# The first stage of a Fourier-and-SwiGLU kernel: an input transfer, matmul order and small sign operations moved

## The chip, the cores and the metric

The kernel runs on one core of a Trainium2 chip. The metric is the device time of one execution in microseconds; the median of three runs is given, and one further execution was taken by the hardware profiler. A core has a tensor engine (PE; its weight loads are listed as PEld), a vector engine (DVE, VectorE), a scalar engine (ACT, ScalarE), GpSimd (POOL) and a sync engine (SP) that issues most transfers. Each engine works through its own queue in order and waits for the others by semaphores.

## The reference

`x` has 8 batches of 3008 rows and 256 columns. Its two-dimensional Fourier transform is taken in each batch and the real part goes through a SwiGLU block of width 1536:

```python
X = np.fft.fft(x, axis=1)
X = np.fft.fft(X, axis=2)
x = X.real.reshape(B * S, D)
g = x @ w_gate
v = x @ w_val
return (g / (1 + np.exp(-g)) * v) @ w_out
```

## The kernel before

**The idea.** The transforms are matrix products with cosine and sine tables that the kernel makes itself. The transform along the columns is folded into the weights: `Wp` and `Wq` are the gate and value weights times a cosine and a sine matrix (`CD`, `SDt`), and `Wm` is `Wq` with a factor for the mirrored rows. The transform along the rows uses the symmetries of the tables: rows that stand opposite each other are added and subtracted first ("folding"), in quarters of a batch, so that a batch needs a fraction of the products. What comes out is held in two bf16 tiles per block of up to 512 rows, `Pt` (even part) and `Qt` (odd part); a row and its mirrored row come from `Pt` and `Qt` with the sum and the difference.

**Units.** The work behind the first stage is a list of units (t, f): row block t and 128 of the 1536 columns, f from 0 to 11. In the blocks whose kind is "w" (block 0, all of it) a unit is: gate product (`Wp` times `Pt`, then `Wq` times `Qt`, L1033), value product likewise, silu on ACT (L1068), the product `hp` of silu and value on DVE (L1071); then `Wm` times `Qt` is added to gate and value in place (L1033 again), silu (L1089), and the product `hm` (L1092). So a unit's second value product has to wait until L1071 has read the first. The output product is L1297. A small planner in the kernel (`Sched`) takes the units' operations with the costs written beside them and due times and works out one order for each engine ahead of time; the order is then fixed. The costs that it is given don't change with what an operation's function issues.

**The first stage** (up to about 18 us) is written out by hand. It loads batch 0, makes the tables, folds, and does the first half of batch 0's row transform so that block 0 can start.

- The rows of a batch quarter are cut in two parts, "A" (128 rows) and "C" (the other 60, and the middle rows). Part A comes into `XA`, part C into `XC0`. Falling rows have to be turned round; batch 0 does that on PE: a placing matrix (`putA`, `putC`, made by an iota and a compare on POOL, L411 and L412, `more_iotas` and L415) times the rows (L442). `XC0` is cleared by ACT (L300), then filled by SP's transfers (L274, L277) and by one small transfer from POOL's queue, L416: the middle rows, 4 KB.
- The folding of part C is on DVE: L449 and L450 (`cross_halves`), L460 (`half_fold`), L454 (`ends`); then L588 makes a part of the odd rows of A (`EOb`).
- PE's row products go into four accumulators, `acc[eo][q]`, eo even or odd, q the column half: `half_folded` (L485, part A), `folded_c` (L490, part C), `row0` (L634, the zero row). `even_copy` (L514, ACT) copies the accumulator of column half 0, and `first_puts` (L652, DVE) adds and subtracts it from that of half 1 and writes `Pt` (eo 0) or `Qt` (eo 1).
- `first_w` (L502) makes the first 512 columns of `Wp` and `Wq`; ACT and DVE copy them out (L505).
- Weights come by POOL's queue, `load_w` (L403): it converts to bf16 on the way. The parts for later columns are turned into `Wp` and `Wq` among the units (`weight_op`: L1519 on PE, casts L1522, L1525 and L1528, the `Wm` part on POOL, L1534).
- `heads` (L464, L465, POOL) and `row_signs` (L366, L367, POOL), with the two small products of L676, make the coefficients of single columns and rows: the signs of part C. `turn_signs` (L355 to L357, DVE) makes four signs per partition, `turn_sign`, which are read at L1586 when the second half of the odd table is made from the first half.

Among the units of block 0 stand the operations that make the odd tables (`before`, L1636): `turns` (L373, POOL), `angles` (L377, DVE), `magnitude` (L381, DVE), sine and cosine (L384, L387, ACT), the quarter rows of part A (L1564 to L1568, POOL). `magnitude_op(0)` and `magnitude_op(1)` are added at unit 3, each with a cost of 0.35.

Of the kernel before, what the change touches and what calls it, by code (L numbers as in the profile page):

```python
# [16 lines left out]
Alu = mybir.AluOpType  # L17

@with_exitstack
def kernel(  # L20
# [8 lines left out]
    nc = tc.nc  # L29
    B, M, D = x.shape  # L30
# [5 lines left out]
    R = M // 4  # L36
# [16 lines left out]
    NCR = GH - P  # L53
# [43 lines left out]
    Ec0 = mEc[:, 4:8].rearrange("p (a q d) -> p a q d", a=2, q=2)  # L97
# [10 lines left out]
    sgn = const.tile([P, 1], F32, name="sgn")  # L108
    nsgn = const.tile([P, 1], F32, name="nsgn")
# [15 lines left out]
    rrO = XA.rearrange("p a q d -> p (a q d)")[:, 4 * T:4 * T + 4 * GH].rearrange("p (c q n) -> p c q n", c=2, q=2)  # L125
# [5 lines left out]
    def rows_at(b, row, ap):  # L131
        return bass.AP(tensor=x.tensor, offset=(b * M + row) * D, ap=ap)
# [84 lines left out]
    def coef_a(b):  # L217
        if b not in coefA:
            coefA[b] = (cp.tile([P, 2, 2, 2, P + 1], BF16, name="CEa"),
                        cp.tile([P, 2, 2, 2, P], BF16, name="BBa"))  # L220
        return coefA[b]

    def stack(b):
        if b not in stacks:
            stacks[b] = stp.tile([P, 4 * ND], BF16, name="St")
        return stacks[b]
# [11 lines left out]
    pts = nc.gpsimd.tensor_scalar  # L238
# [8 lines left out]
    XC0 = tp.tile([P, 4, 2, D], F32, name="XC0")  # L247
# [58 lines left out]
    def more_iotas():  # L306
        nc.gpsimd.memset(putC, -1.0)
        for hi in range(2):
            pm = 64 * hi + NCR
            nc.gpsimd.iota(putC[:, pm - NCR:pm], pattern=[[-2 * LC, NC_], [2, LC]], base=2 * (NCR - LC) + hi, **iota)  # L310
# [42 lines left out]
    def turn_signs():  # L353
        n_ = turn_sign.bitcast(I32)
        vts(n_, mm_, scalar1=0.5, scalar2=0.25, op0=Alu.mult, op1=Alu.add)  # L355
        vts(n_, n_, scalar1=1, scalar2=None, op0=Alu.bitwise_and)
        vts(turn_sign, n_, scalar1=-2.0, scalar2=1.0, op0=Alu.mult, op1=Alu.add)  # L357
# [7 lines left out]
    def row_signs():  # L365
        pts(sgo, pc, scalar1=float(NCR), scalar2=-2.0, op0=Alu.is_equal, op1=Alu.mult)  # L366
        pts(sgo, sgo, scalar1=1.0, scalar2=sgn, op0=Alu.add, op1=Alu.mult)  # L367
# [3 lines left out]
    def turns(t1, kf, ch):  # L371
        for i in range(2):
            pts(t1[:, i, :], kf, scalar1=mM[:, 2 * ch + i:2 * ch + i + 1], scalar2=1.0, op0=Alu.mult, op1=Alu.mult)  # L373
# [6 lines left out]
    def magnitude(ra, rr):  # L380
        vts(ra.bitcast(I32), rr.bitcast(I32), scalar1=0x7FFFFFFF, scalar2=None, op0=Alu.bitwise_and)  # L381
# [16 lines left out]
    def load_w(c, only):  # L398
        for i, src in ((0, moe_w_gate), (1, moe_w_val)):
            if i not in only:  # L400
                continue
            w_ = src.rearrange("(no p) f -> p no f", p=P)[:, :, c * T:(c + 1) * T]
            nc.gpsimd.dma_start(out=Wraw[i][:, :, (c - 1) * T:c * T] if c else W0[i], in_=w_)  # L403
# [3 lines left out]
    BBc = stack(0)[:, 0:8 * P].rearrange("p (q e k d) -> p q e k d", q=2, e=2, k=2)  # L407
# [3 lines left out]
    nc.gpsimd.iota(putA, pattern=[[-LA, NA], [1, LA]], base=JA - 1, **iota)  # L411
    pts(putA, putA, scalar1=pcol, scalar2=1.0, op0=Alu.is_equal, op1=Alu.mult)  # L412
    turns(ti[1], kf, 1)
    more_iotas()
    pts(putC, putC, scalar1=pcol, scalar2=1.0, op0=Alu.is_equal, op1=Alu.mult)  # L415
    nc.gpsimd.dma_start(out=XC0[NCR:64 + NCR + 1:64, 2:4, 0], in_=rows_at(0, 0, [[2 * R * D, 2], [R * D, 2], [1, D]]))  # L416
    ce_angle = [[tp.tile([P, 2, NCE], F32, name=f"{nm}{ch}") for nm in ("rr", "ra")] for ch in range(2)]
    tp.tile([P, 4404], F32, name="pad")

# [42 lines left out]
    def heads(ev, od, CE):  # L462

        ptt(CE[:, :, 0, 0, -1:], ev, od, op=Alu.add)  # L464
        ptt(CE[:, :, 0, 1, -1:], ev, od, op=Alu.subtract)  # L465
# [9 lines left out]
    def set_cols(ps, tab, a):  # L475
        if a % 2:
            return (ps[:, 0:2 * GH + 2].rearrange("p (t n) -> p t n", t=2),
                    tab[:, 0:2 * NCE].rearrange("p (t n) -> p t n", t=2)[:, :, 0:GH + 1])
        return ps[:, 0:NCE], tab[:, 0:NCE]

    def half_folded(eo, a0, first, qs=(0, 1)):
        for q in qs:
            for a in range(a0, a0 + 2):
                dst, rhs = set_cols(acc[eo][q], Tab[:, 0, q, eo], a)
                nc.tensor.matmul(dst, EOb[:, eo, a, q, :], rhs, start=first and a == a0, stop=False, skip_group_check=True)  # L485

    def folded_c(eo, a, first=False):
        for q in range(2):
            dst, rhs = set_cols(acc[eo][q], Tab[:, 1, q, eo], a)
            nc.tensor.matmul(dst, EB[:, eo, a, q, :], rhs, start=first and a == 0, stop=a == 1, skip_group_check=True)  # L490
# [21 lines left out]
    def even_copy(eo):  # L512
        od = odp.tile([P, NCE], F32, name="od")
        nc.scalar.copy(od, acc[eo][0][:, 0:NCE])  # L514
        return od
# [70 lines left out]
    half_fold(1, EB[:, 1, 1], FC[:, 1], psC[1])  # L586
    for i in range(2):
        vtt(EOb[:, 1, 0:2, i], EOA[1][0][:, :, i], EOA[1][1][:, :, i], op=Alu.add)  # L588
    heads(Ec0[:, 0], Ec0[:, 1], CEc)
    load_w(1, (1,))  # L590
    half_folded(0, 2, False)
    folded_c(0, 0)
    copies = [first_w(0, k, 1, one_bank(k)) for k in range(2)]
# [31 lines left out]
    def row0(b, q, ps):  # L625
        if b:
            for k, (c, e) in enumerate(((0, E0), (0, E1), (1, slice(0, NCE)))):
                nc.tensor.matmul(ps[:, e], Z0[:, q, k, :], Tab[:, c, q, 0, e], start=False, stop=True,  # L628
                                 skip_group_check=True)
            return  # L630
        CE = coef_a(b)[0]
        for c, head in ((0, CE[:, q, 0, :, P:P + 1]), (1, CEc[:, q, 0])):
            for k, e in ((0, E0), (1, E1)):
                nc.tensor.matmul(ps[0:1, e], head[:, k, :], Tab[:, c, q, 0, e], start=False, stop=True,  # L634
                                 skip_group_check=True)
# [11 lines left out]
    def first_puts(eo, od, tiles):  # L647
        for c0, s0, minus in ((0, 1, 0), (GH, 0, 1), (G, GH + 1, 0), (G + GH, GH + 1, 1)):
            for t, off, src, w in pieces(c0, GH):
                if t in tiles:  # L650
                    s_ = slice(s0 + src, s0 + src + w)
                    vtt(pq_tiles(t)[eo][:, off:off + w], acc[eo][1][:, s_], od[:, s_], op=SUMS[minus])  # L652
        if 1 in tiles:
            vtt(last[eo][:, 0:1], acc[eo][1][:, 0:1], od[:, 0:1], op=Alu.add)
# [3 lines left out]
    first_puts(0, od0, (0, 1))  # L658
    for c in copies:
        c()  # L660
    half_folded(1, 0, False)
    for i in range(2):
        row0(0, i, acc[1][i])
        if i == 0:
            od1 = even_copy(1)
# [2 lines left out]
    first_puts(1, od1, (0,))  # L668
    copies[1]()
    first_puts(1, od1, (1,))  # L670
    turn_signs()
    tmp_ctx.close()
    first_ctx.close()
    row_signs()
    for k in range(2):
        pts(BBc[:, :, 1, k, 0:1], Ec0[:, 1 - k], scalar1=(nsgn, sgn)[k], scalar2=1.0, op0=Alu.mult, op1=Alu.mult)  # L676
    nc.gpsimd.iota(kfO, pattern=[[4, GH]], base=1, **iota)
    nc.gpsimd.memset(sel[0:1, :], 1.0)

# [355 lines left out]
    S = Sched()  # L1035
# [513 lines left out]
    raO = SDf.rearrange("p a d -> p (a d)")[:, 0:4 * GH].rearrange("p (c q n) -> p c q n", c=2, q=2)  # L1549
# [4 lines left out]
        S.add("DVE", 0.75, lambda: angles(rrO[:, ch], kfO, ch, turned), r=[(("A",), "pre"), (("kfO",), 0)], w=[(("rr",), ch)])  # L1554

    def magnitude_op(ch):
        S.add("DVE", 0.35, lambda: magnitude(raO[:, ch], rrO[:, ch]), r=[(("rr",), ch), (("A",), "pre")],
              w=[(("ra",), ch), (("fold",), "F")])

    def quarters_op():  # L1560
# [72 lines left out]
    def odd_op(i):  # L1633
        S.add("POOL", 1.4, lambda: odd_table(i // 2, i % 2), r=[(("Tab",), ("o", 1))], w=[(("Tab",), "k")])

    before = {0: [lambda: angle_op(0)], 1: [lambda: angle_op(1)], 2: [lambda: weight_op(1, 0)], 3: [lambda: weight_op(1, 1), lambda: magnitude_op(0), lambda: magnitude_op(1)],  # L1636
              4: [lambda: weight_op(2, 0), lambda: cosine_op(0)], 6: [quarters_op, odd_ends_op], 5: [lambda: weight_op(2, 1), lambda: cosine_op(1)],
              7: [lambda: sine_op(0), rows_op], 8: [lambda: sine_op(1)], 9: [weigh_op, lambda: second_half_op(0), lambda: second_half_op(1)],
# [56 lines left out]
    for i, u in enumerate(units):  # L1695
# [25 lines left out]
        if i == RESCALE:  # L1721
            state["scaled"] = True
            S.add("ACT", 1.3, lambda: nc.scalar.activation(Wm[:, 1], Wm[:, 1], AF.Copy, scale=-0.5),
                  r=[(("Wm",), (fc, 1)) for fc in range(3)], w=[(("Wm",), 1)])
# [58 lines left out]
```

## Time and profile before

| | us |
|---|---|
| median of three runs | 598.26 |
| the three runs | 597.51, 598.26, 598.62 |
| profiled execution, its own time | 597.96 |
| span of the profiled execution (first to last instruction) | 596.2 |
| PE busy | 590.3 (99%) |
| DVE / ACT / POOL busy | 569.2 / 553.6 / 533.1 |
| first matmul of a unit (L1033) starts | 18.26 |

The granted TensorE clock is 1.00 in every stage. A row of the timeline gives the start in us from the beginning of the span, the duration (of the whole group where it says xN), the engine, the line, the operation, output and input tiles with their shapes, and in brackets the idle time of the engine just before and what ended it. A row of the waits gives the waiting engine and line, what it waited for, the us in total, how often, and the longest. In the chain of the work that ended last each row is a piece with its start and length; "issue" is time in which the profile shows nothing that the engine waited for.

### The profile page before, as it was taken

The page shows a single profiled execution, that of the slowest core. Times are in us where ns is not written, and L with a number is a line of the kernel's source. Part 1 is how long each engine was busy: PE and PEld are TensorE (multiplying, and loading weights), DVE is VectorE, ACT ScalarE, POOL GpSimd, SP SyncE. Part 2 cuts the span into 40 slices and gives each one's busy share as a digit, 9 for nine tenths or more (in the row PEclk, how much of TensorE's full clock was granted, in tenths as well). Part 3 has the DMA queues.
Part 4 walks back from the last instruction along what each step waited for, and adds up shares of the span by engine and source line. Part 5 has one row for each costly group of instructions (what it writes and reads, how often), then busy time and mean ns, then how long its engine had stood idle before and what let it go on. Part 6 is the DMA issues. An engine that isn't in the chain of part 4 may idle for free.

```text
span 596.2 us, 12375 instructions
## 1 busy us (share of the span) xinstructions
PE 590.3 (99%) x4001; PEld 388.7 (65%) x4001; DVE 569.2 (95%) x1063; ACT 553.6 (93%) x1071; POOL 533.1 (89%) x491
## 2 busy tenths in 40 slices
PE   8999999999999999999999999999999999999997
PEld 5456666666666666666666666666666666666686
DVE  8989999999999999999999999999999999999993
ACT  8768989999999899999999999999999999999995
POOL 8989999999999999999899998999889868687782
PEclk9999999999999999999999999999999999999999
DMA  8966772756243255275225122063121103202212
GB/s 244 166 219 234 189 230 71 195 165 220 83 151 126 70 144 132 54 254 165 81 79 171 37 63 64 19 182 113 47 63 37 47 19 89 66 29 63 60 54 81
DMA packets 61086, 68.17 MB, mean 114 GB/s; under 512 B 6760, under 2 KB 48684, under 8 KB 61022
## 3 DMA queue, kind: packets, MB, share of 16 engines
q1 hardware_dynamic: 57438, 64.44, 36.1%
q0 software_dynamic: 3216, 2.36, 2.8%
q8 instruction: 31, 0.51, 0.4%
q10 hardware_dynamic: 368, 0.59, 0.3%
q14 instruction: 33, 0.27, 0.1%
HBM read 40.21 MB, written 35.43 MB: 127 GB/s over the span
## 4 chain that ended last, share of the span: by engine, by line
PE 95%; DMA 1%; POOL 1%; SPq 1%; DVE 0%; ACT 0%; issue 0%; ACTq 0%; POOLq 0%
PE o L1297 40%; PE g L1033 27%; PE v L1033 21%; PE g L1471 2%; PE o L1471 2%; PE v L1297 1%; DMA XC<-in_x_dram 1%; DMA out_dram<-ev 1%; PE o L1519 1%; POOL t L373 0%; PE g L628 0%; PE o L628 0%; SPq L1310 0%; PE b L502 0%; PE b L490 0%
## 5 line engine op out<-in xcount | busy, mean ns | idle before, releaser
L1244 POOL TENSOR_TENSOR hm<-sv 128x1024 bf16<-128x1024 f32 (+2 forms) x137 | 254.7, 1862 | 32.7 <-ACT sv L1220 16.8
L1236 DVE SCALAR_TENSOR_TENSOR sv<-es,v 128x512 f32<-128x512 f32 (+2 forms) x262 | 174.5, 672 | 6.2 <-PE v L1033 4.3
L1297 PE MATMUL o<-Wo,hm 128*128 128x256 bf16 (+1 forms) x1128 | 163.7, 273 | 0.0
L1297 PE MATMUL o<-Wo,hp 128*128 128x256 bf16 (+1 forms) x1104 | 161.1, 272 | 0.0
L1247 DVE TENSOR_TENSOR hp<-sp,v 128x512 bf16<-128x512 f32 (+2 forms) x228 | 152.0, 673 | 1.8 <-PE v L1033 1.0
L1297 PEld LDWEIGHTS <-hm 128*128 128x128 bf16 (+2 forms) x1140 | 111.9, 98 | 58.0 <-issue 0.6
L1297 PEld LDWEIGHTS <-hp 128*128 128x128 bf16 (+2 forms) x1140 | 111.9, 98 | 55.4 <-issue 0.6
L1220 ACT ACTIVATE sv<-g 128x512 f32<-128x512 f32 (+2 forms) x181 | 118.4, 672 | 3.7 <-PE g L1033 3.2
L1145 ACT ACTIVATE sp<-g 128x512 f32<-128x512 f32 (+2 forms) x181 | 111.6, 618 | 6.1 <-PE g L1033 4.5
L1033 PE MATMUL g<-Pt,Wp 128*128 128x512 bf16 (+2 forms) x288 | 107.5, 374 | 0.0
L1033 PE MATMUL v<-Pt,Wp 128*128 128x512 bf16 (+2 forms) x288 | 106.2, 374 | 0.0
L1033 PE MATMUL g<-Qt,Wq 128*128 128x512 bf16 (+2 forms) x288 | 105.4, 375 | 0.0
L1106 ACT ACTIVATE v<-bc,w 128x512 f32<-128x512 bf16 (+2 forms) x139 | 99.7, 721 | 1.7 <-DVE sv L1236 0.9
L1170 DVE SCALAR_TENSOR_TENSOR es<-bc,w,v 128x512 f32<-128x512 bf16 (+2 forms) x135 | 98.1, 734 | 2.1
L1168 ACT ACTIVATE es<-v 128x512 f32<-128x512 f32 (+2 forms) x139 | 85.4, 617 | 3.3 <-PE v L1033 1.5
L1033 PE MATMUL g<-Qt,Wm 128*128 128x512 bf16 (+2 forms) x195 | 73.1, 376 | 0.0
L1033 PEld LDWEIGHTS <-Wp 128*128 128x128 bf16 x576 | 56.3, 98 | 25.2 <-issue 0.3
L1149 DVE SCALAR_TENSOR_TENSOR sg<-bc,w,g 128x512 f32<-128x512 bf16 (+2 forms) x93 | 67.5, 726 | 1.6 <-PE g L1033 1.4
L1253 POOL TENSOR_TENSOR hp<-sp,pp 128x512 bf16<-128x512 f32 (+1 forms) x46 | 57.1, 1245 | 8.0 <-ACT pp L1250 7.8
L1220 ACT ACTIVATE sv<-sg 128x512 f32<-128x512 f32 (+2 forms) x93 | 63.4, 693 | 0.5 <-POOL hp L1253 0.5
L1213 DVE SCALAR_TENSOR_TENSOR sg<-sg,g 128x512 f32<-128x512 f32 (+2 forms) x93 | 61.8, 665 | 0.2
L1033 PEld LDWEIGHTS <-Wq 128*128 128x128 bf16 x437 | 42.7, 98 | 28.4 <-issue 1.3
(201 smaller groups left out, 781.8 us busy)
## 6 DMA issues: line engine op xcount, KB each, us to landing
out_dram<-ev SPq DMA_DIRECT2D x96, 128.0 KB
XA<-in_x_dram SPq DMA_DIRECT2D x30, 256.0 KB
tA<-in_x_dram SPq DMA_DIRECT2D x28, 256.0 KB
XA<-tA SPq DMA_DIRECT2D x14, 512.0 KB
XC<-in_x_dram SPq DMA_DIRECT2D x28, 120.0 KB
tC<-in_x_dram SPq DMA_DIRECT2D x28, 120.0 KB
XC<-tC SPq DMA_DIRECT2D x6, 480.0 KB
bc<-br SPq DMA_DIRECT2D x19, 128.0 KB
```

Source lines behind the costliest of these rows:

```text
L1033: nc.tensor.matmul(ps[:, :n], Wt[:, gv, fs], src[:, :n], start=start, stop=stop, skip_group_check=True)
L1106: nc.scalar.activation(T_[kv][:, :w], bc[t][:, :w], AF.Copy, scale=w0[:, 1, f:f + 1])
L1145: nc.scalar.activation(sp_to()[:, :w], T_[kg][:, :w], AF.Silu)
L1149: nc.vector.scalar_tensor_tensor(T_[keg][:, :w], bc[t][:, :w], w0[:, 0, f:f + 1], T_[kg][:, :w], op0=Alu.mult, op1=Alu.add)
L1168: nc.scalar.activation(T_[kes][:, :w], T_[kv][:, :w], AF.Copy, scale=2.0 if on_pool(u) > 1 else 1.0)
L1170: nc.vector.scalar_tensor_tensor(T_[kes][:, :w], bc[t][:, :w], w0[:, 1, f:f + 1], T_[kv][:, :w], op0=Alu.mult, op1=Alu.add)
L1213: nc.vector.scalar_tensor_tensor(T_[kgm][:, :w], T_[keg][:, :w], 2.0, T_[kg][:, :w], op0=Alu.mult, op1=Alu.subtract)
L1220: nc.scalar.activation(sv()[:, f % 2, w - 1::-1, 1], T_[kgm if by_dve else kg][:, :w], AF.Silu)
L1236: nc.vector.scalar_tensor_tensor(sv()[:, f % 2, w - 1::-1, 0], T_[kes][:, :w], 2.0, T_[kv][:, :w], op0=Alu.mult, op1=Alu.subtract)
L1244: nc.gpsimd.tensor_tensor(hts_(t)[1][:, f - 1:f + 1, :w], sv()[:, :, :w, 1], sv()[:, :, :w, 0], op=Alu.mult)
L1247: nc.vector.tensor_tensor(hts_(t)[0][:, f, :wp], T_[ksp][:, :wp], T_[kv][:, :wp], op=Alu.mult)
L1297: nc.tensor.matmul(st["ps"][:n, j, :], hts[t][minus][:, f, c:c + n], Wo[:, f, :], start=(f == 0), stop=(f == nF - 1))
```

## The change

Four things are moved; nothing is computed otherwise.

1. L416, the middle rows' transfer, is issued on POOL before `more_iotas` and L415, not behind them.
2. `half_folded(1, 0, ...)` is called for one column half at a time, each followed by its `row0`; before, both halves came first. The copy `even_copy(1)` stays behind the first `row0`.
3. `row_signs` is issued before `heads`, and the two products of L676 between the fourth and the last two of `load_w`'s transfers; before, all four stood at the end of the stage, ahead of the iota `kfO`.
4. `turn_signs` is no longer at the end of the stage; its three DVE operations are issued right behind the first magnitude (L381, channel 0), at unit 3, within the same planned operation.

```diff
     turns(ti[1], kf, 1)
+    nc.gpsimd.dma_start(out=XC0[NCR:64 + NCR + 1:64, 2:4, 0], in_=rows_at(0, 0, [[2 * R * D, 2], [R * D, 2], [1, D]]))
     more_iotas()
     pts(putC, putC, scalar1=pcol, scalar2=1.0, op0=Alu.is_equal, op1=Alu.mult)
-    nc.gpsimd.dma_start(out=XC0[NCR:64 + NCR + 1:64, 2:4, 0], in_=rows_at(0, 0, [[2 * R * D, 2], [R * D, 2], [1, D]]))
...
+    row_signs()
     heads(Ec0[:, 0], Ec0[:, 1], CEc)
     load_w(1, (1,))
+    for k in range(2):
+        pts(BBc[:, :, 1, k, 0:1], Ec0[:, 1 - k], scalar1=(nsgn, sgn)[k], scalar2=1.0, op0=Alu.mult, op1=Alu.mult)
     half_folded(0, 2, False)
...
-    half_folded(1, 0, False)
     for i in range(2):
+        half_folded(1, 0, False, (i,))
         row0(0, i, acc[1][i])
         if i == 0:
             od1 = even_copy(1)
...
-    turn_signs()
     tmp_ctx.close()
     first_ctx.close()
-    row_signs()
-    for k in range(2):
-        pts(BBc[:, :, 1, k, 0:1], Ec0[:, 1 - k], scalar1=(nsgn, sgn)[k], scalar2=1.0, op0=Alu.mult, op1=Alu.mult)
     nc.gpsimd.iota(kfO, pattern=[[4, GH]], base=1, **iota)
...
     def magnitude_op(ch):
-        S.add("DVE", 0.35, lambda: magnitude(raO[:, ch], rrO[:, ch]), r=[(("rr",), ch), (("A",), "pre")],
+        S.add("DVE", 0.35, lambda: (magnitude(raO[:, ch], rrO[:, ch]), ch or turn_signs()), r=[(("rr",), ch), (("A",), "pre")],
               w=[(("ra",), ch), (("fold",), "F")])
```

## The prediction

> **What bounds the kernel now.** I read the head of the profile's page first, then the waits of the tensor engine, then the chain of work that ended last, then the timeline of the first 31 us engine by engine.
>
> ```profile
> span 596.2 us, 12375 instructions
> PE 590.3 (99%) x4001; PEld 388.7 (65%) x4001; DVE 569.2 (95%) x1063; ACT 553.6 (93%) x1071; POOL 533.1 (89%) x491
> ...
> PE v L1033 <- DVE hp L1071: 0.5, 1, 0.5
> PE b L490 <- DVE EOf L460: 0.4, 1, 0.4
> ```
>
> PE is the bound. The list of its waits has four rows (line, releaser, us in total, times, longest); three belong to the first stage, as the second one shown here, and the only one behind it is the 0.5 us at L1033. So a microsecond by which PE's stream comes earlier or later before about 31 us stands unchanged in the end time: behind it PE has no idle time that could swallow a delay, and none that a gain could come from. The question is only how the start and the first units move. Of them these rows (start, us, engine, line) carry the argument:
>
> ```profile
> 6.10 0.20 POOL L307 MEMSET putC<- 128x128 f32 x1
> ...
> 6.92 0.94 POOL L415 TENSOR_SCALAR putC<-putC,pcol 128x128 f32<-128x128 f32 x1
> 7.81 0.81 POOL L416 DMA_DIRECT2D XC<-in_x_dram  x1
> ...
> 7.81 3.83 DMA XC<-in_x_dram
> 11.64 0.40 issue
> ```
>
> The chain hangs on POOL's queue up to the issue of the middle rows (L416), then on that transfer, and VectorE stands idle for 0.40 us, from 11.64, until it starts L449 at 12.04.
>
> **Part 1, the transfer ahead of the matrix.** L416 starts at 6.10 in place of 7.81, ahead of L307, the two iotas and L415. These four come 0.81 later: L415 ends at 8.67 in place of 7.86. The matmul that reads putC starts at 9.41 (row below), so 0.74 us of cover are left; the weight issue L403 behind the five stays where it is. No other queue's order changes. With the same 4.2 us (7.81 to 12.04) the rows are there at 10.3, before VectorE is free at 11.64. It can then start L449 at about 11.6: gain at most 0.45 us, nothing if another of the XC transfers, whose landing no row shows, is as late. I take 0.4, because the chain names this transfer and no other.
>
> The Trainium skill, page "SBUF — State Buffer", section "SBUF: two separate sides", warns that GpSimd cannot write the descriptors of a transfer while VectorE runs an operation on both of its ports. By it L416 at 6.10, beside VectorE's angle operations, could be stretched to about 7.7 and the gain would be near 0.1 in place of 0.4; that is rival 3 below by another way.
>
> **Part 2, by column half.**
>
> ```profile
> 9.41 1.96 PE L442 MATMUL b<-XC,putC 128*128 128x512 f32 x4
> ...
> 15.87 0.83 PE L485 MATMUL b<-Tab,EOb 128*128 128x377 bf16 x4
> 16.63 0.33 PE L634 MATMUL b<-Tab,CEa 128*1 128x189 bf16 x2
> ...
> 17.13 0.33 PE L634 MATMUL b<-Tab,CEc 128*1 128x189 bf16 x2
> 17.39 0.60 PE L502 MATMUL b<-W,CD 128*128 128x512 bf16 x2
> ...
> 18.26 0.57 PE L1033 MATMUL g<-Pt,Wp 128*128 128x480 bf16 x2
> 17.67 0.35 DVE L652 TENSOR_TENSOR Qt<-b,od 128x188 bf16<-128x188 f32 x1 [0.34 <-ACT od L514]
> ```
>
> The same eight and four matmuls run in another order, so that the copy L514 can start two L485 matmuls (some 0.4 us) earlier. But L652 reads both halves, and PE's last L634 pair ends at 17.46 (17.13 + 0.33): at most 17.67 - 17.50 = 0.17 is won. Against it, the step from the last L634 pair to L502 took 0.26 where a pair takes 0.17 (three in 17.13 - 16.63), and the new order has two such changes of kind more: 0.18 lost. Net nothing, bounds 0.17 either way. Both parts together: L1033 starts at about 17.9 in place of 18.26, 0.35 gained (bounds 0.1 and 0.6).
>
> **Part 3, row signs by the heads.**
>
> ```profile
> 15.20 0.20 POOL L464 TENSOR_TENSOR CEc<-mEc 128x2 bf16<-128x2 f32 x1 [0.54 <-DVE mEc L454]
> ...
> 17.94 0.25 POOL L366 TENSOR_SCALAR sgo<-pc 128x1 f32<-128x1 f32 x1
> ...
> 19.01 0.28 POOL L677 IOTA EOf<- 128x188 f32 x1
> ...
> 15.68 0.73 POOL L403 DMA_DIRECT2D XA<-in_moe_w_val_dram  x1
> ...
> XA<-in_moe_w_val_dram POOLq DMA_DIRECT2D x1, 256.0 KB, 6.5
> ...
> 23.02 0.59 PE L1519 MATMUL o<-XA,CD 128*128 128x512 bf16 x2
> ```
>
> Four POOL instructions (L366, L367, L676 twice) fill 17.94 to 19.01, 1.07 us. Their new place begins in the 0.54 us in which POOL waits for the heads, so some 0.4 are hidden, and the last two weight issues (L403 again) come about 0.65 later. A landing later by these 0.65 costs at most a part of the lead that PE has by then, nothing against before. What follows on POOL (L677, L678, L509) comes about 0.5 us earlier. The weight issue ahead of them stays at 15.68; with its 6.5 us it lands at 22.2, and L1519 reads it at 23.02: PE cannot be more than 0.8 us ahead of before there, whatever else is won.
>
> **Part 4, turn signs.** This decides.
>
> ```profile
> 3.60 1.17 DVE L377 SCALAR_TENSOR_TENSOR rr<-kf,mM,t 128x377 f32<-128x377 f32 x2
> ...
> 5.64 1.44 DVE L377 SCALAR_TENSOR_TENSOR rr<-kf,mM,t 128x377 f32<-128x377 f32 x2
> ...
> 19.55 0.60 DVE L355 TENSOR_SCALAR turn_sign<-mEc 128x4 int32<-128x4 f32 x1
> 20.18 0.63 DVE L356 TENSOR_SCALAR turn_sign<-turn_sign 128x4 int32<-128x4 int32 x1
> 20.85 0.36 DVE L357 TENSOR_SCALAR turn_sign<-turn_sign 128x4 f32<-128x4 int32 x1
> 21.12 1.21 DVE L1071 TENSOR_TENSOR hp<-sg,v 128x480 bf16<-128x480 f32 x2
> ...
> 24.15 0.64 DVE L1092 TENSOR_TENSOR hm<-sg,v 128x480 bf16<-128x480 f32 x1
> ...
> 25.84 0.64 DVE L381 TENSOR_SCALAR SDf<-XA 128x376 int32<-128x376 int32 x1
> 26.40 0.64 DVE L1071 TENSOR_TENSOR hp<-sg,v 128x480 bf16<-128x480 f32 x1
> 26.96 0.34 DVE L381 TENSOR_SCALAR SDf<-XA 128x376 int32<-128x376 int32 x1
> ...
> 19.43 1.36 POOL L509 TENSOR_SCALAR Wm<-Wq,m 128x512 bf16<-128x512 bf16 x2
> 20.77 1.60 POOL L373 TENSOR_SCALAR XA<-EOf,mM 128x188 int32<-128x188 f32 x4
> ...
> 24.84 0.68 POOL L1534 TENSOR_SCALAR Wm<-Wq,m 128x512 bf16<-128x512 bf16 x1 [0.74 <-ACT Wq L1528]
> 25.50 0.72 POOL L1564 TENSOR_TENSOR BBa<-Af,XA 128x256 bf16<-128x256 f32 x1
> ...
> 26.23 0.83 POOL L1565 TENSOR_TENSOR BBa<-XA,Af 128x256 bf16<-128x256 f32 x1
> 27.04 0.82 POOL L1534 TENSOR_SCALAR Wm<-Wq,m 128x512 bf16<-128x512 bf16 x1
> 27.83 1.26 POOL L1567 TENSOR_TENSOR BBa<-Fc 128x512 bf16<-128x512 f32 x1
> ...
> 27.09 0.36 PE L1033 MATMUL v<-Qt,Wm 128*128 128x480 bf16 x1
> ```
>
> Four elements a partition need no 0.6 us. Set beside POOL's rows the reason shows: L356 ends at 20.82, just behind the second L509 (20.79); L355 ends at 20.15, behind the first of the pair (19.43 + 0.68 = 20.11); L357 ends at 21.21, one L373 (0.40) behind 20.77. Each sign operation lasts until the POOL instruction beside it is done. The two L381 agree: the same work takes 0.64 with L1564 beside it (ends 26.22) and 0.34 when L1565 is nearly done (27.06). And as each sign operation reads the one before, POOL's next instruction has started when the next one comes, and it waits for all of that too.
>
> The Trainium skill, page "SBUF — State Buffer", section "SBUF: two separate sides", says so too: VectorE in a two-port mode and GpSimd hold a shared port exclusively, for a whole instruction, and the other blocks fully. The trace agrees, with the ends named above. By that rule moving the three operations saves nothing where POOL is busy.
>
> What is removed: 1.57 us of VectorE (19.55 to 21.12), and PE's wait for L1071, the 0.5 of the waits list. L1071 then starts at about 19.45 (19.55 less the 0.35, and a quarter of a microsecond for ScalarE's silu, an estimate), and PE runs 0.8 us ahead of before, as far as the weights let it, up to 26 us.
>
> What is added: L381, three signs and then L1071, whose result PE's L1033 at 27.09 waits for (26.40 + 0.64 = 27.04). VectorE shows no idle time in its rows from 21.12 to 26.96, so a delay here is paid by PE at once. The cost of the three: beside an idle POOL next to nothing, and no more than three times the 0.34 that L381 took for 376 elements; beside a busy one at most what is left of one POOL instruction and two or three whole ones. Walking it: with L1071 at 19.45 the cast and the angles (L377, four of them, beside POOL's L373 now, where the pair at 5.64 took 1.44 against 1.17 at 3.60) end between 22.6 and 23.3, and the first L381 comes, 1.69 behind L1092, at 24.2 to 24.9 in place of 25.84. POOL's L1534 waits for ScalarE's cast, hence for PE, and comes at 24.0; from there L1564, L1565, L1534 and L1567 follow without a gap. With L381 at 24.9: it waits for L1564 and ends at 25.6; L1565 then ends at 26.3 and the first sign behind it, L1534 at 26.9 and the second, L1567 at 28.1 and the third. L1071 starts at 28.1, not 26.40: **1.7 us late**. With L381 at 24.2 everything is one instruction earlier, the last wait is for L1534, and L1071 starts at 26.9: 0.5 late. I take the first, for the angles stood beside POOL's L373 in the rows named and lost time there. Up to 2.0 is possible, if L381 comes later still.
>
> PE then has lost its lead and 1.7 us more at that matmul, and there is nothing behind it where it could catch up.
>
> **Sum.** The profiled execution took 597.96 (span 596.2 and 1.76 around it). The start's 0.35, the 0.5 and the lead up to 0.8 are used up in the wait for L1071; what remains is its lateness: 597.96 + 1.7 = 599.66, so **599.7 us**. The median of the runs shown is 598.26, 0.30 above the profiled execution, and they reach from 597.51 to 598.62; 0.3 of this goes into the range at the upper end.
>
> **The rivals.**
> 1. *One POOL instruction fewer in the way*: the angles are not held up, or a sign operation gets through at the small memset between L1564 and L1565. L1071 is 0.1 to 0.5 late: 598.1 to 598.5. For it: the walk misses such a gap by less than 0.1 us. Against: in the old place all three lost.
> 2. *Faster*: the signs run beside an idle POOL. The row of L1534 shows 0.74 us in which POOL waits for ScalarE; if L381 and the signs fall there, they cost 1.0 at most, and L1071 is still ahead of before. It decides where L381 starts before POOL's L1534 has its data. PE keeps 0.6 to 0.9 of its lead: 597.1 to 597.4. Against: that L1534 comes at 24.0, 0.8 earlier with PE's lead, and VectorE, which comes 0.9 to 1.6 earlier, would have to reach L381 1.8 us earlier.
> 3. *The transfer is not the last of its kind* (or lands later): no gain at the start, so VectorE comes to the signs 0.35 later than forecast and L1071 with it, or one POOL instruction on. 599.7 to 600.2. Against: the chain names this transfer alone.
>
> **Chances.** Forecast 0.48 (599.2 to 600.3 by itself), rival 1 0.25, rival 2 0.22, rival 3 0.05. A measurement of this kernel tells about 0.2% (1.2 us) from no change: below 597.06 is faster, above 599.46 slower. Half of rival 2 with its spread lies below: 0.12. Forecast and rival 3, less the forecast's lower end: 0.48. The rest, 0.40, is the same. For 8 in 10 the range reaches from 597.3 (rival 2's middle) to 600.6 (2.0 late and the 0.3 of the runs).
>
> **What would show it.** Part 1: no idle time before the first L449, which starts at 11.6. Part 2: L652 at about 17.2 with no more gap than now. Part 3: L509 near 18.9. Part 4: L355 to L357 behind the first L381, each ending just behind a POOL instruction, together over 1.5 us; the third L1071 behind 27 us; a new row of PE's waits, L1033 for L1071, of over 1 us. It is wrong if the three signs take under 0.6 us together, or if PE does not wait there.

## The result, and the profile after

The changed kernel takes 599.13 us (median of 19 runs, 598.62 to 599.65); the kernel before takes 598.11 us on the same chip (19 runs, 597.51 to 598.78). The ratio is 1.0016, with a 95% interval of 1.0009 to 1.0023: 1.0 us slower, 0.5 to 1.4. The forecast was 599.7. The profiled execution took 598.71 us, against 597.96 before.

In after.py the lines of the units stand one lower than in the code above (L1033 is L1032, L1071 is L1070, L1092 is L1091, L1534 is L1533, L1567 is L1566, L1600 is L1599); L652 is L655, L634 is L637, the products of L676 are L593, and the transfer L416 is L414. The experiments have the lines of the units by the one count or the other, and number POOL's quarter rows and signs (L1564, L1567, L1629) in the same way. Every row shown is of the one profiled execution of its kernel.

First the page's head and PE's waits, to be held against those of before:

```profile
span 596.9 us, 12376 instructions
...
PE v L1032 <- DVE hp L1070: 1.0, 1, 1.0
PE v L1032 <- DVE hm L1091: 0.4, 2, 0.2
```

The one wait behind the first stage was 0.5 us for hp; now it is 1.0 for hp and 0.4 for hm (two waits of 0.2), and none of the listed waits of 0.2 us or more lies behind them. Then the first stage, from the timeline:

```profile
6.10 0.80 POOL L414 DMA_DIRECT2D XC<-in_x_dram  x1
...
11.50 0.41 DVE L449 TENSOR_TENSOR FC<-b,XC 128x256 f32<-128x256 f32 x1
...
17.24 0.79 DVE L655 TENSOR_TENSOR Qt<-b,od 128x188 bf16<-128x188 f32 x3 [0.52 <-PE b L637]
...
17.94 0.57 PE L1032 MATMUL g<-Pt,Wp 128*128 128x480 bf16 x2
```

The reader is to see the gain shrink from row to row: L449 0.54 us earlier than before (12.04) and with no idle time ahead of it, the sums of Qt 0.43 (17.67), the first product 0.32 (18.26). And then the units, in the same view, VectorE's and POOL's rows and the PE rows that wait for them:

```profile
19.14 1.36 POOL L509 TENSOR_SCALAR Wm<-Wq,m 128x512 bf16<-128x512 bf16 x2
19.48 1.22 DVE L1070 TENSOR_TENSOR hp<-sg,v 128x480 bf16<-128x480 f32 x2 [0.17 <-ACT sg L1067]
20.48 1.60 POOL L373 TENSOR_SCALAR XA<-EOf,mM 128x188 int32<-128x188 f32 x4
21.21 2.48 DVE L377 SCALAR_TENSOR_TENSOR XA<-EOf,mM,XA 128x188 f32<-128x188 f32 x4
22.06 0.77 POOL L1533 TENSOR_SCALAR Wm<-Wq,m 128x512 bf16<-128x512 bf16 x1
...
25.30 0.72 POOL L1564 TENSOR_TENSOR BBa<-XA,Af 128x256 bf16<-128x256 f32 x1
25.31 0.93 DVE L381 TENSOR_SCALAR SDf<-XA 128x376 int32<-128x376 int32 x1
...
26.16 0.15 DVE L355 TENSOR_SCALAR turn_sign<-mEc 128x4 int32<-128x4 f32 x1
26.35 0.17 DVE L356 TENSOR_SCALAR turn_sign<-turn_sign 128x4 int32<-128x4 int32 x1
26.39 0.69 POOL L1533 TENSOR_SCALAR Wm<-Wq,m 128x512 bf16<-128x512 bf16 x1 [0.37 <-ACT Wq L1527]
26.55 0.55 DVE L357 TENSOR_SCALAR turn_sign<-turn_sign 128x4 f32<-128x4 int32 x1
27.01 0.64 DVE L1070 TENSOR_TENSOR hp<-sg,v 128x480 bf16<-128x480 f32 x1
27.05 1.26 POOL L1566 TENSOR_TENSOR BBa<-Fc 128x512 bf16<-128x512 f32 x1
27.57 0.96 DVE L381 TENSOR_SCALAR SDf<-XA 128x376 int32<-128x376 int32 x1
27.70 0.36 PE L1032 MATMUL v<-Qt,Wm 128*128 128x480 bf16 x1 [1.02 <-DVE hp L1070]
28.45 0.64 DVE L1091 TENSOR_TENSOR hm<-sg,v 128x480 bf16<-128x480 f32 x1
...
29.15 0.36 PE L1032 MATMUL v<-Pt,Wp 128*128 128x480 bf16 x1 [0.24 <-DVE hm L1091]
...
31.49 0.75 PE L1599 MATMUL o<-sel,Wq 1*128 1x1 bf16 x24
```

hp at 19.48 is 1.64 us earlier than before (21.12), as the forecast had it (19.45). The four angles L377 took 1.37 us before and take 2.48 here, beside L373 and L1533. The three signs take 0.87 (0.15 + 0.17 + 0.55): two of them started in the 0.37 us in which POOL waits for ScalarE (26.02 to 26.39) and were not held, the third ends at 27.10, just behind L1533's end (27.08). hp at 27.01 is 0.61 late, and so is PE (27.70 against 27.09). Then the second magnitude L381 takes 0.96 where it took 0.34, and ends at 28.53, behind L1566's end (28.31): hm is 1.22 late (27.23 before, 28.45 here), and the products L1599 as well (31.49 against 30.27).

That L1599 is the best ruler here: a matmul group that every kernel of this study runs in the same place of PE's order. From it to the end of the span pass 565.4 us in the changed kernel and 565.9 in the profiled execution of before, which therefore lost 0.5 us more behind it, 0.3 of it between 258 and 262 us (the starts of PE's matmuls set side by side in their order). Hence 0.75 us between the two profiled executions, and 1.0 between the medians.

### The profile page after: what moved, and what is told of

Read it like the earlier page. It is cut to its first block, busy times and chain, and to the rows that moved or that the text cites. A ratio compares the mean times of both kernels' runs of the same rounds, so it can differ in the third digit from the quotient of the medians.

```text
span 596.9 us, 12376 instructions
## 1 busy us (share of the span) xinstructions
PE 590.5 (99%) x4001; PEld 388.5 (65%) x4001; DVE 570.2 (96%) x1063; ACT 553.5 (93%) x1071; POOL 533.5 (89%) x491
## 4 chain that ended last, share of the span: by engine, by line
PE 97%; DVE 1%; POOL 0%; issue 0%; ACT 0%; DVEq 0%; POOLq 0%
PE o L1296 41%; PE g L1032 27%; PE v L1032 21%; PE g L1470 2%; PE o L1470 2%; PE v L1296 1%; PE b L442 1%; PE o L631 0%; PE g L631 0%; PE o L1518 0%; PE b L502 0%; PE b L485 0%; PE b L490 0%; PE g L1296 0%; DVE hm L1091 0%
## 5 line engine op out<-in xcount | busy, mean ns | idle before, releaser
L1243 POOL TENSOR_TENSOR hm<-sv 128x1024 bf16<-128x1024 f32 (+2 forms) x137 | 254.7, 1862 | 33.2 <-ACT sv L1219 17.2
L1032 PE MATMUL g<-Pt,Wp 128*128 128x512 bf16 (+2 forms) x288 | 107.5, 374 | 0.0
L1032 PE MATMUL v<-Pt,Wp 128*128 128x512 bf16 (+2 forms) x288 | 106.2, 374 | 0.4 <-DVE hm L1091 0.4
L1032 PE MATMUL g<-Qt,Wq 128*128 128x512 bf16 (+2 forms) x288 | 105.4, 375 | 0.0
L1032 PE MATMUL g<-Qt,Wm 128*128 128x512 bf16 (+2 forms) x195 | 73.1, 376 | 0.0
L1032 PEld LDWEIGHTS <-Wp 128*128 128x128 bf16 x576 | 56.3, 98 | 25.1 <-issue 0.2
L1032 PEld LDWEIGHTS <-Wq 128*128 128x128 bf16 x437 | 42.7, 98 | 28.5 <-issue 1.4
```

What stands on the lines that cost most here:

```text
L1032: nc.tensor.matmul(ps[:, :n], Wt[:, gv, fs], src[:, :n], start=start, stop=stop, skip_group_check=True)
L1243: nc.gpsimd.tensor_tensor(hts_(t)[1][:, f - 1:f + 1, :w], sv()[:, :, :w, 1], sv()[:, :, :w, 0], op=Alu.mult)
```

## The experiments

Theory A: the loss comes from VectorE operations that are held until the GpSimd instruction beside them ends, the signs and the second magnitude above all, while the first three parts gain some 0.3 us. Rival B: only the three signs' own 0.87 us, wherever they stand among the units. Rival C: one of the first three parts loses. The table gives all runs. "ratio" is to the kernel before on the same chip; it is taken from all executions and can differ from the quotient of the medians (for part_4 that is 1.0023). "products" is the start of L1599 or L1600 in the timeline of each run's one profiled execution (before: 30.27, after: 31.49), "first" that of the first product (before: 18.26, after: 17.94).

| run | median us (before's) | ratio, 95% | first | products |
|---|---|---|---|---|
| parts_123 | 597.79 (597.59) | 1.0003, 0.9994 to 1.0012 | 17.92 | 30.37 |
| part_4 | 598.96 (597.59) | 1.0015, 1.0006 to 1.0024 | 17.92 | 31.67 |
| signs_in_gap | 597.48 (597.59) | 0.9997, 0.9988 to 1.0006 | 17.93 | 30.23 |
| signs_second | 599.39 (597.59) | 1.0029, 1.0018 to 1.0041 | 18.10 | 32.21 |
| part_1 | 598.29 (597.82) | 1.0005, 0.9996 to 1.0013 | 17.78 | 29.99 |
| gap_rows_behind | 597.92 (597.82) | 0.9997, 0.9989 to 1.0006 | 17.85 | 30.45 |
| gap_rows_old | 598.17 (597.82) | 1.0005, 0.9996 to 1.0013 | 18.08 | 29.88 |
| quarters_9 | 597.75 (597.82) | 0.9997, 0.9989 to 1.0006 | 18.04 | 30.35 |
| part_2 | 597.57 (597.67) | 1.0000, 0.9991 to 1.0008 | 18.49 | 30.34 |
| part_3 | 598.13 (597.67) | 1.0012, 1.0002 to 1.0022 | 17.86 | 31.32 |
| gap_quarters | 597.08 (597.67) | 0.9992, 0.9984 to 1.0001 | 18.02 | 29.80 |
| part_1_gap_quarters | 598.07 (597.67) | 1.0003, 0.9995 to 1.0012 | 17.75 | 29.73 |

### Without the fourth part, and the fourth part alone

parts_123 is the changed kernel with this edit; part_4 is the kernel before with the opposite one.

```diff
     first_puts(1, od1, (1,))
+    turn_signs()
...
-        S.add("DVE", 0.35, lambda: (magnitude(raO[:, ch], rrO[:, ch]), ch or turn_signs()), r=[(("rr",), ch), (("A",), "pre")],
+        S.add("DVE", 0.35, lambda: magnitude(raO[:, ch], rrO[:, ch]), r=[(("rr",), ch), (("A",), "pre")],
```

> The change without its fourth part: the turn signs stand where they stood before, at the end of the first stage. Theory A (the loss comes from Vector operations of the units that are held by the GpSimd instruction beside them; the first three parts gain what the trace after shows, 0.3 us at the first product): the signs wait for L509 as before, which starts 0.29 us earlier, so all of the units start 0.3 us earlier; time about 0.3 us under the kernel before (0.1 to 0.5 under). Rival C (the first three parts lose): 0.2 us or more above the kernel before.

> The kernel before with the fourth part alone: the turn signs behind the first magnitude. Theory A: the first product of hp comes some 1.3 us earlier, but the angles, the signs and the second magnitude meet the GpSimd instructions as in the changed kernel; time 1.0 to 1.5 us above the kernel before. Rival B (only the signs' own 0.87 us at their new place cost, and the 1.6 us at the old one are gained): no more than 0.5 us above. Rival C: 0.7 us or more below it would leave the loss with the other parts.

The fourth part alone gives the loss of the whole change: 1.0015, and products 1.40 us late. That speaks against rival C for this change. But its eleven times fall into two groups, five from 597.82 to 598.14 us and six from 598.96 to 599.52; the profiled execution (599.05) belongs to the second. So the 1.40 us stand for the second group; the first group loses only 0.2 to 0.6 us against before's median; it has no trace. But the other three together gain nothing: 1.0003, products 0.10 late, although the first product is 0.34 early. The timeline of parts_123 shows where it went:

```profile
19.12 1.36 POOL L509 TENSOR_SCALAR Wm<-Wq,m 128x512 bf16<-128x512 bf16 x2
...
19.22 1.31 DVE L355 TENSOR_SCALAR turn_sign<-mEc 128x4 int32<-128x4 f32 x1
20.47 1.60 POOL L373 TENSOR_SCALAR XA<-EOf,mM 128x188 int32<-128x188 f32 x4
...
21.21 1.20 DVE L1071 TENSOR_TENSOR hp<-sg,v 128x480 bf16<-128x480 f32 x2
```

The first sign waited for both instructions of L509, the other two for an L373 each, and hp starts at 21.21, with before's 21.12. In this execution the queue of POOL, not the start, sets the time at the signs' old place; my 0.3 us was wrong there.

### The signs at two other places

signs_in_gap is parts_123 with the first edit, signs_second the changed kernel with the second.

```diff
+    turn_signs()
     copies[0]()
     first_puts(1, od1, (0,))
     copies[1]()
     first_puts(1, od1, (1,))
-    turn_signs()
```

```diff
-        S.add("DVE", 0.35, lambda: (magnitude(raO[:, ch], rrO[:, ch]), ch or turn_signs()), r=[(("rr",), ch), (("A",), "pre")],
+        S.add("DVE", 0.35, lambda: (magnitude(raO[:, ch], rrO[:, ch]), (1 - ch) or turn_signs()), r=[(("rr",), ch), (("A",), "pre")],
```

> The changed kernel with the turn signs ahead of the first sums of tile 0's Qt, in the gap of 0.52 us that Vector has there; nothing is behind the magnitude. Theory A: with the signs gone from the magnitude's place, the second magnitude comes 0.7 us earlier and meets L1533 and then L1566 of GpSimd, and is held until about 28.5 us as in the changed kernel if GpSimd keeps the turn from one instruction to the next; time 0.7 to 1.2 us above the kernel before, so no gain on the changed kernel. If the magnitude gets in between the two, it is 0.3 us under to 0.1 above the kernel before. Rival B (the signs' duration alone): 0.87 us under the changed kernel, 0.1 us above the kernel before, with the second magnitude held no less than in the changed kernel.

> The changed kernel with the turn signs behind the second magnitude in place of the first. Theory A: there they follow the magnitude that is held by L1566 (1.26 us) and stand beside L1626 twice, each held by the instruction beside it; the second hm comes 0.5 to 1.5 us later than in the changed kernel; time 1.3 to 2.5 us above the kernel before. Rival B: the same 0.87 us at another place, so the time of the changed kernel, 1.0 us above the kernel before, within 0.2.

In signs_in_gap the signs end at 17.31 and delay nothing. The second magnitude did get in between L1534 and L1567, the milder of the two cases that I had named:

```profile
26.38 0.69 POOL L1534 TENSOR_SCALAR Wm<-Wq,m 128x512 bf16<-128x512 bf16 x1 [0.37 <-ACT Wq L1528]
26.72 0.56 DVE L381 TENSOR_SCALAR SDf<-XA 128x376 int32<-128x376 int32 x1
27.04 1.36 POOL L1567 TENSOR_TENSOR BBa<-Fc 128x512 bf16<-128x512 f32 x1
27.20 0.64 DVE L1092 TENSOR_TENSOR hm<-sg,v 128x480 bf16<-128x480 f32 x1
```

It ends at 27.28, 0.21 behind L1534's end (27.07). Time and products are those of before (0.9997; 0.04 early). This run does not separate A from B by its time, though B had expected the second magnitude to be held no less than in the changed kernel. signs_second separates them: 1.0029, products 1.94 us late, against 1.22 in the changed kernel. The same three operations, behind the second magnitude, cost more:

```profile
27.21 1.36 POOL L1566 TENSOR_TENSOR BBa<-Fc 128x512 bf16<-128x512 f32 x1
27.37 1.22 DVE L355 TENSOR_SCALAR turn_sign<-mEc 128x4 int32<-128x4 f32 x1
...
29.87 0.36 PE L1032 MATMUL v<-Pt,Wp 128*128 128x480 bf16 x1 [1.65 <-DVE hm L1091]
```

L355 alone, four elements a partition, lasts 1.22 us and ends at 28.59, with L1566 (28.57). The three now take 1.81 us (1.22 + 0.42 + 0.17) in place of 0.87. A fixed cost of the signs (rival B) cannot do that.

### POOL's instructions moved, the signs left where the change puts them

quarters_9 is the changed kernel with this edit of the list of what is planned ahead of which unit.

```diff
-              4: [lambda: weight_op(2, 0), lambda: cosine_op(0)], 6: [quarters_op, odd_ends_op], 5: [lambda: weight_op(2, 1), lambda: cosine_op(1)],
-              7: [lambda: sine_op(0), rows_op], 8: [lambda: sine_op(1)], 9: [weigh_op, lambda: second_half_op(0), lambda: second_half_op(1)],
+              4: [lambda: weight_op(2, 0), lambda: cosine_op(0)], 6: [odd_ends_op], 5: [lambda: weight_op(2, 1), lambda: cosine_op(1)],
+              7: [lambda: sine_op(0), rows_op], 8: [lambda: sine_op(1)], 9: [quarters_op, weigh_op, lambda: second_half_op(0), lambda: second_half_op(1)],
```

> The changed kernel, with GpSimd's four quarter sums (L1563 to L1567) moved three units later in its order; Vector's and PE's orders are untouched, the turn signs stay behind the first magnitude. Theory A (Vector's signs and magnitudes are held by the GpSimd instruction beside them): the first magnitude meets L1626 only (0.47 us), the signs fall into GpSimd's idle time ahead of L1533 and take 0.5 us, the second magnitude does not meet L1566; the second hm comes near 27.4 us in place of 28.45, and the time is 0.1 under to 0.4 above the kernel before. Rival B (the signs' own duration at this place): the time of the changed kernel, 0.8 to 1.2 above the kernel before.

```profile
25.20 0.47 POOL L1626 TENSOR_SCALAR St<-EOf,nsgn 128x256 bf16<-128x256 bf16 x1
25.43 0.45 DVE L381 TENSOR_SCALAR SDf<-XA 128x376 int32<-128x376 int32 x1
25.80 0.15 DVE L355 TENSOR_SCALAR turn_sign<-mEc 128x4 int32<-128x4 f32 x1
...
26.19 0.17 DVE L357 TENSOR_SCALAR turn_sign<-turn_sign 128x4 f32<-128x4 int32 x1
...
26.84 0.56 DVE L381 TENSOR_SCALAR SDf<-XA 128x376 int32<-128x376 int32 x1
...
27.32 0.64 DVE L1091 TENSOR_TENSOR hm<-sg,v 128x480 bf16<-128x480 f32 x1
```

Nothing of VectorE's or PE's order changed, and the loss is gone: 0.9997 where the changed kernel has 1.0016, products 30.35 in place of 31.49 (before 30.27). The signs take 0.56 us from 25.80 on (the last ends at 26.36), beside an idle POOL; hm comes at 27.32, as forecast. Rival B expected the time of the changed kernel and falls. This shows the cause: not the signs, but what POOL does beside them and beside the two magnitudes.

### Each of the first three parts alone

> The kernel before with the first part alone. L449 on the middle rows starts some 0.5 us earlier and the first product 0.3 us earlier, but the turn signs, still at the end of the first stage, wait for the same GpSimd L509 (19.4 to 20.8 us) as before, so that the second product of hp starts near 21.1 us as before. Theory A: the gain at the start is gone behind the signs, 0.0 within 0.15 us by the trace, 0.3 under to 0.3 above by the times. By the prediction's term it would be 0.3 to 0.4 us under the kernel before.

> The kernel before with the second part alone: the odd products and row products of the second stage half by column half. By the prediction's step (net nothing, 0.17 us either way) the first product of Pt and Wp starts at 18.26 within 0.17 us. By the runs so far, in which L449 on the middle rows to the first product takes 6.21 us (kernel before), 6.20 (first part alone), 6.34 to 6.38 (second part, row signs later) and 6.44 (the changed kernel), the split itself costs 0.15 us: first product near 18.4. Either way hp waits for the turn signs and these for L509, so the time is that of the kernel before, within 0.3.

> The kernel before with the third part alone: the row signs and their products earlier, ahead of the DMA of the W values. By the prediction's step L509 starts 0.5 us earlier (near 18.9) and nothing else moves. The turn signs at the end of the first stage then end 0.3 to 0.5 us earlier if they get in between L509's two instructions (as in the run with the first part alone), and the time is 0.2 to 0.5 us under the kernel before; if they meet the turns L373 behind L509 (as in the run of the first three parts) it is the same within 0.2.

(Each is the kernel before with the lines of that part from the diff above.) part_1: the first product 0.48 earlier, and hp too, at 20.64, since here the first sign got in between the two L509; the products are 0.28 early. The time is nevertheless not less (1.0005), and it is lost much later:

```profile
40.06 2.35 POOL L187 TENSOR_TENSOR SDf<-XC 128x1020 f32<-128x1020 f32 x1 [3.10 <-DMA XC<-tC]
...
59.63 0.65 ACT L1220 ACTIVATE sv<-g 128x512 f32<-128x512 f32 x1 [0.74 <-POOL hm L1244]
...
60.89 0.38 PE L1033 MATMUL v<-Pt,Wp 128*128 128x512 bf16 x1 [0.68 <-ACT v L1106]
```

Read it upwards: PE waits for ScalarE, ScalarE for POOL's hm, and POOL is late because L187, the first folding of a later batch, waited 3.10 us for a transfer (XC from tC); from there to that hm the timeline lists a single idle time of POOL, 0.21 us. So the waits list of before is misleading in one point: PE is full behind 31 us only as long as it comes late enough; a second limit lies close behind. Where L187 starts 9.95 us or more behind L1600 (part_1, gap_rows_old, part_1_gap_quarters), PE waits there; 9.33 (part_2) costs next to nothing, and 9.04 or less nothing. (The expectations count L187 from a record 1.4 us ahead of the timeline's row; the differences are the same.) Those three runs have in common that the transfer of the middle rows is early and the row signs are not: the three weight transfers L403 are then issued at 15.2 to 16.8 us and those for the value weights take 8.5 to 8.8 us from issue to landing (median of two); in the kernel before they are issued at 15.7 to 17.1 and take 7.7, in the changed kernel at 15.9 to 18.0 and take 6.0. part_4, without the first part, issued them as early (15.3 to 16.8) and had 8.3 us; its L187 started as late (39.57), but so did its products, and PE did not wait. That the weight transfers crowd out those for L187 fits this; it was not tried.

part_2: first product at 18.49, 6.39 us behind its L449 (12.10), where before has 6.22 (18.26 - 12.04): the split costs 0.17, the lower bound of the forecast. In the time it is nothing (1.0000). part_3 came out slower, 1.0012, against both things that I expected, and again in two groups: six of its twelve times lie from 597.41 to 597.69 us, those of before, and six from 598.58 to 600.72. The profiled execution (598.81) belongs to the second:

```profile
19.15 0.83 DVE L355 TENSOR_SCALAR turn_sign<-mEc 128x4 int32<-128x4 f32 x1
19.27 1.36 POOL L509 TENSOR_SCALAR Wm<-Wq,m 128x512 bf16<-128x512 bf16 x2
...
20.02 1.44 DVE L356 TENSOR_SCALAR turn_sign<-turn_sign 128x4 int32<-128x4 int32 x1
20.61 1.61 POOL L373 TENSOR_SCALAR XA<-EOf,mM 128x188 int32<-128x188 f32 x4
...
22.15 1.21 DVE L1071 TENSOR_TENSOR hp<-sg,v 128x480 bf16<-128x480 f32 x2
```

L509 is 0.16 earlier, the signs meet six POOL instructions in a row (two L509, four L373; the last sign began at 21.49), and hp starts 1.03 late. In this execution the loss is again at the signs, now at their old place; what the first group does there no trace shows.

### The row signs elsewhere

> Turn signs in the gap ahead of Qt's sums, and the row signs behind the heads that PE's row products read (CEc) in place of ahead of them. In the changed kernel PE waits 0.31 us at L637 for these heads, which are behind the two row signs. If that wait is on the path to the first product, the first product comes 0.2 to 0.3 us earlier than with the signs in the gap alone and the time is 0.3 to 0.6 us under the kernel before. If Vector's Qt sums are late for another reason, it is the same as with the signs in the gap, 0.1 to 0.3 under.

> As the one before, but the row signs and their two products stand where the kernel before has them, ahead of the iota for the odd columns: the third part undone. The first product comes as early as in the run with the row signs behind the heads; L509 and the turns L373 come 0.2 to 0.4 us later, and the angles L377 with them. If these do not bound (PE waits 0.2 us there), the time is that of the run with the row signs behind the heads, within 0.15; if they do, 0.2 to 0.4 us above it.

gap_rows_behind is signs_in_gap with this edit; gap_rows_old is signs_in_gap with row_signs and its two products (L593) back ahead of the iota kfO.

```diff
-    row_signs()
     heads(Ec0[:, 0], Ec0[:, 1], CEc)
+    row_signs()
     load_w(1, (1,))
```

The heads were no gate: with the row signs behind them the first product came at 17.85, 0.08 earlier, not 0.2 to 0.3 (and L449 alone was 0.06 earlier, 11.51 against 11.57). The first magnitude, beside two POOL instructions, lasted 1.26 us and lost the gain again (products 30.45). gap_rows_old has its products earlier (29.88) and lost that at the second limit (1.0005). Neither beats signs_in_gap.

### Towards a better version

> The changed kernel with the turn signs in Vector's gap ahead of Qt's sums and the quarter sums three units later. Neither the signs nor L1564 and L1566 stand beside a Vector instruction of the units 3 to 5 that PE waits for; PE's waits for hp and hm between 26 and 29 us go, and the row products (L1600) come 0.3 to 0.6 us earlier than in the kernel before (29.7 to 29.95 us). Theory A: 0.3 to 0.6 us under the kernel before. A second limit may show: where GpSimd's L187 waits for a DMA until over 8.3 us behind L1600 (8.66 and 8.52 with a wait of PE near 60 us, 7.4 and less without), PE loses up to 0.8 us there, and the time is that of the kernel before.

> The kernel before with the first part, the turn signs ahead of Qt's sums and the quarter sums three units later; the second and third part are not in it. If these two cost what the starts say (0.24 us together), L1600 comes 0.1 to 0.3 us earlier than in the run with all of the change's first three parts; the time is 0.4 to 0.8 us under the kernel before. The second limit (L187's DMA, the wait of PE near 60 us) is nearer here: where it bites, the time is that of the kernel before or 0.3 us above.

gap_quarters is signs_in_gap with the quarter sums at unit 9:

```profile
25.41 0.45 DVE L381 TENSOR_SCALAR SDf<-XA 128x376 int32<-128x376 int32 x1
25.78 0.64 DVE L1071 TENSOR_TENSOR hp<-sg,v 128x480 bf16<-128x480 f32 x1
...
26.34 0.34 DVE L381 TENSOR_SCALAR SDf<-XA 128x376 int32<-128x376 int32 x1
...
26.61 0.64 DVE L1092 TENSOR_TENSOR hm<-sg,v 128x480 bf16<-128x480 f32 x1
...
29.80 0.75 PE L1600 MATMUL o<-sel,Wq 1*128 1x1 bf16 x24
```

The magnitudes take 0.45 and 0.34 (free: 0.34), hm is 1.84 us earlier than in the changed kernel, the products 0.47 earlier than before. The time is 597.08 against 597.67, ratio 0.9992, 0.9984 to 1.0001: faster than the changed kernel, and by 0.6 us lower in the median than before, though the interval still holds one. part_1_gap_quarters, without the second and third part, has its products at 29.73, earliest of all, and falls to the second limit: 1.0003. Its profiled execution, the longest of its eleven (598.62; the shortest took 597.18), loses 0.58 us at 60 us and about as much again at a third place:

```profile
260.03 0.59 ACT L1304 COPY ev<-o 128x512 f32<-128x512 f32 x1 [0.83 <-DMA out_dram<-ev]
...
261.16 0.38 PE L1033 MATMUL v<-Qt,Wm 128*128 128x512 bf16 x1 [0.70 <-ACT es L1168]
```

ScalarE's copy waited for a transfer out, the es behind it came late, and PE waited for that. It is the stretch in which the kernel before lost its 0.3 us. The two kernels differ in the second and third part; which of the two keeps L187's transfer early was not tried alone.

## Why the prediction was right, point by point

- **Bound.** "Earlier or later before about 31 us stands unchanged in the end time": for a delay this held within the 0.5 us by which the stretch behind L1599 differs. For a gain it did not; part_1 lost its own at 60 us.
- **Part 1.** Forecast: L449 at 11.6, gain 0.4. Measured 11.50, gain 0.54. But two runs without this part started it at 11.69 (part_3) and 11.71 (part_4), and the ten with it between 11.50 and 11.74, so the part is worth between nothing and 0.6 us, by the execution of before that it is held against. The issue row of the transfer took 0.80 us (0.81 before): VectorE's operations beside it did not stretch it.
- **Part 2.** Net nothing, bounds 0.17: measured 0.17 lost alone, and 0.22 in the changed kernel (6.44 us from L449 to the first product, before 6.22), just outside the bound. L655 came at 17.24 (forecast 17.2), but its gap was 0.52 us and not the 0.34 of before.
- **Part 1 and 2 together.** 17.9 forecast for the first product, 17.94 measured; the larger gain of the one and the loss of the other cancelled, which is luck.
- **Part 3.** "No cost" held in the changed kernel; L509 came at 19.14, not 18.9, since L366 took 0.52 us beside VectorE's L588. The limit by the weights (a lead of 0.8 us) did not show in the changed kernel, but part_4's waits list has it:

```profile
PE o L1518 <- DMA XA<-in_moe_w_val_dram: 0.3, 1, 0.3
```

- **Part 4.** The mechanism was right, that VectorE is held by the POOL instruction beside it and PE pays, but the term that decided was mis-sized: "L1071 starts at 28.1, not 26.40: 1.7 us late". It started at 27.01, 0.61 late. The walk had the first L381 at 24.2 to 24.9; the angles were held longer than the forecast's range (to 23.69, not 22.6 to 23.3), so it came at 25.31, behind that range, and two of the signs then fell into POOL's wait for ScalarE; rival 1 had looked for such a gap at the memset, rival 2 ahead of L1534. The forecast had sized the angles by 1.44 against 1.17 us at the start, as if only the slower pair stood beside POOL; but beside the faster one (from 3.60) ran POOL's L412 (3.63 to 4.74). By L1071 alone the run is nearer to rival 1 (0.1 to 0.5 late) than to the forecast, and of what the forecast named as its marks one is missing: L355 to L357 took 0.87 us together, not over 1.5, and one of the three, not each, ended just behind a POOL instruction. L1071 behind 27 us (27.01) and PE's wait of over 1 us (1.02) came, both barely. What brought the time near to the forecast all the same is a collision of the same kind that the forecast left out: it ended the walk at L1071 and took the second L381 for free, and that lost 0.62 us to L1566. 0.61 and 0.61 more make the 1.22 at the products. That the two errors nearly cancel is luck.
- **Sum.** 1.7 by the forecast, 1.22 at the products, 1.0 (0.5 to 1.4) between the medians. The direction rests on less luck than the size: part_4, with another alignment in its profiled execution (two of the signs held, 0.68 + 0.20 + 0.48 us), gives 1.40 at the products and 1.0015.
- **The parts do not add.** Alone they move the products by -0.28, +0.07, +1.05 and +1.40 us; together by +1.22. With the signs gone from the old place the third part has nothing there to push them into. That is not all of it: the first three together (parts_123) move the products by 0.10 only, with the signs still there, so what the signs meet turns on a tenth or two of a microsecond (L355 started 0.10 us behind L509 there, and 0.12 ahead of it in part_3, where it was held as well and the next sign longer).

The Trainium skill, page "SBUF — State Buffer", section "SBUF: two separate sides", has whichever of VectorE's two-port operation and GpSimd's instruction starts first hold the shared port for a whole instruction. That VectorE's operation waits for the end of POOL's agrees with the ends named above. But one would read from it that L355 of parts_123, waiting since 19.22, has its turn when the first of the two L509 (0.68 us each) ends at 19.80; it lasted until 20.53, behind the end of both (20.48), so GpSimd can keep the port. In part_1 (L355, 19.07 to 19.67, the first L509 until 19.63) and in signs_in_gap the waiting operation did get in between. What decides between the two was not found.

## What to carry to other kernels

Before a small VectorE operation is moved, read the rows of GpSimd at its new place. Here its price was not its length (0.15 us free) but what was left of the GpSimd instruction beside it, or of two in a row (up to 1.44 us), and the operations behind it paid again where they were pushed beside other GpSimd instructions. Follow the walk past the moved operation until the rows agree with before again. It can be cheaper to move GpSimd's instruction than VectorE's (quarters_9 won back all of the loss). And look for the second limit before counting on a gain: that the tensor engine is full says only that nothing else is late yet (part_1 won 0.28 us at its products and lost it at 60 us). Where the times of one kernel fall into groups, look which of them the profiled execution belongs to.

## What the runs showed that was not expected

- A magnitude of 376 elements a partition took 0.34 us free, 0.43 to 0.96 beside one GpSimd instruction and 1.26 beside two; a sign operation on four elements 0.15 to 1.44.
- GpSimd is held as well: L366 took 0.52 us in the changed kernel and 0.25 before, L1567 1.36 in signs_in_gap and 1.26 before.
- A gain at the start of 0.3 to 0.5 us can turn into nothing 40 us later through a transfer that no wait of PE shows in the kernel before.
- With the 4 KB transfer issued at the old place, L449 started at 11.69 and 11.71 us right behind VectorE's work in two executions (part_3, part_4), and at 12.04 and 12.10 after idle time in two others (before, part_2): the start of L449, and with it most likely the landing, varies by as much as the first part was to win.
